# A causal convolution and a three-way maxout FFN in one kernel: merged tail blocks, six weight staging buffers, casts moved to GpSimd, and a new order of the stages

## The chip, the cores and the metric

The kernel runs on one core of a Trainium2 chip. The metric is the device time of one execution in microseconds (us); lower is better. Spans in the profile are about 2 us shorter than the measured time.

Engine names: PE is TensorE, DVE is VectorE, ACT is ScalarE, POOL is GpSimd, SP is SyncE (it only issues transfers here).

## The reference

```python
# x (8, 4160, 192) f32, weight (8, 7); moe_w1..w3 (192, 768), moe_w_out (768, 192)
w = softmax(weight, axis=-1)                              # 8 heads x 7 taps
# causal depthwise convolution, one 7-tap filter per head of 24 channels
out = einsum('hk,bskhg->bshg', w, windows_of_7(x))        # (8, 4160, 192)
x = out.reshape(33280, 192)
h = maximum(maximum(x @ w1, x @ w2), x @ w3)              # (33280, 768)
return h @ w_out                                          # (33280, 192)
```

4160 is 8 x 512 + 64.

## The kernel before

Work goes in blocks of up to 512 rows. For each block:

1. A transfer brings x in, and ACT casts it to fp16.
2. PE does the convolution as 40 small matmuls against a band matrix (5 chunks of 122 rows, 8 heads) into two PSUM tiles, G1 and G2. ACT casts both to fp16 (xctA, xctB).
3. Stage 1: six slices `j` of 128 hidden columns. Each slice takes six 128x512 matmuls into three PSUM tiles. ACT copies the first, and DVE takes two maxima.
4. Stage 2 of the *previous* block: four subtiles of 128 rows, six matmuls each. ACT copies the result out.

```python
    psg = ctx.enter_context(tc.tile_pool(name="psg", bufs=2, space=bass.MemoryType.PSUM))
    ps1 = ctx.enter_context(tc.tile_pool(name="ps1", bufs=4, space=bass.MemoryType.PSUM))
    ps2 = ctx.enter_context(tc.tile_pool(name="ps2", bufs=2, space=bass.MemoryType.PSUM))
    ...
            stage = wpool.tile([P, DFF], FP32, tag="wstage")      # one buffer, used six times
            nc.vector.memset(stage[:], 0.0)
            ...                                                   # 4 loads into stage
            nc.scalar.copy(out=wt[:], in_=stage[:])
    ...
    for t, (b, S, N) in enumerate(blocks):        # 72 blocks: 8 x (8 of 512 rows, 1 of 64)
        ...                                       # load x, nc.scalar.copy to x16
        ...                                       # 40 convolution matmuls into G1, G2
        nc.scalar.copy(out=xctA[:, 0:N], in_=G1[:, 0:N])
        nc.scalar.copy(out=xctB[:, 0:N], in_=G2[:, 0:N])
        if prev is not None:
            emit_stage2(prev)
        hT = htp.tile([P, NJ, NBLK], FP16, tag="hT")
        for j in range(NJ):
            ...                                   # 6 matmuls into psw[0..2]
            nc.scalar.copy(out=t1[:, 0:N], in_=psw[0][:, 0:N])
            nc.vector.tensor_max(out=t12[:, 0:N], in0=t1[:, 0:N], in1=psw[1][:, 0:N])
            nc.vector.tensor_max(out=hT[:, j, 0:N], in0=t12[:, 0:N], in1=psw[2][:, 0:N])
        prev = (hT, b, S, N)
```

The order of the source is not quite the order on the engines. A scheduler places the instructions when the kernel is built, and each engine then has its own list.

The softmax here doesn't subtract the row's maximum and nothing guards it: scores larger than these inputs give would overflow.

## Time and profile before

| before | value | read from |
|---|---|---|
| time | 806.5 us, median of 4 (806.11 to 807.0) | the times |
| PE busy / DVE busy / ACT busy | 92% / 68% / 55% | the page, part 1 |
| a batch (8 full blocks and a tail) | 94.7 us mean | ACT's casts of G in the timeline |
| its tail of 64 rows | 5.9 us | the same |
| a full block | 11.1 us mean | (94.7 - 5.9) / 8 |
| one slice on PE / on DVE | 1.296 / 1.39 us | the timeline |

From the page of before: the span; the busy times in us, with their share of the span and the number of instructions (PEld is the weight load); and the busy tenths of PE and DVE in 40 slices of 20 us.

```profile
span 804.3 us, 17219 instructions
...
PE 738.2 (92%) x6800; PEld 402.8 (50%) x6800; DVE 543.3 (68%) x943; ACT 439.6 (55%) x945; POOL 0.4 (0%) x5
...
PE   1279999999999999999999999999999999999997
...
DVE  7247766766676677676676667667766666766775
```

PE looks full after the first 40 us. It is not: a 128x512 matmul is drawn 0.38 us long but in an unbroken run the next starts 0.216 us later (402.54 and 402.75 below). The first three digits (1, 2, 7) are the slow start.

The timeline of before, across the end of one full block and the start of the next (start, duration, engine, line, operation, tiles; in brackets the idle time before it and who ended it):

```profile
402.33 0.68 DVE L266 TENSOR_TENSOR t<-t,psw 128x512 f32<-128x512 f32 x1
...
402.54 0.38 PE L249 MATMUL psw<-xctA,wt 128*128 128x512 f16 x1
...
402.75 0.38 PE L256 MATMUL psw<-xctB,wt 128*128 128x512 f16 x1
...
403.07 0.38 PE L249 MATMUL psw<-xctA,wt 128*128 128x512 f16 x1
...
403.12 0.69 DVE L267 TENSOR_TENSOR hT<-t,psw 128x512 f16<-128x512 f32 x1
...
403.72 0.68 DVE L266 TENSOR_TENSOR t<-t,psw 128x512 f32<-128x512 f32 x1
...
404.67 0.38 PE L256 MATMUL psw<-xctB,wt 128*128 128x512 f16 x1
...
404.98 0.65 PE L226 MATMUL G<-band,x 128*32 128x122 f16 x40
...
405.89 0.69 DVE L267 TENSOR_TENSOR hT<-t,psw 128x512 f16<-128x512 f32 x1
...
407.14 0.99 ACT L209 CAST x<-xf 128x960 f16<-128x960 f32 x1
...
408.46 0.61 ACT L265 COPY t<-psw 128x512 f32<-128x512 f32 x1
...
409.10 0.69 DVE L266 TENSOR_TENSOR t<-t,psw 128x512 f32<-128x512 f32 x1 [2.52 <-ACT t L265]
```

Two regimes alternate. Late in a block DVE runs without a gap: from 402.33 to 403.72 is one pair of maxima, 1.39 us, and PE, which could do a slice in 1.296, waits for PSUM that DVE has not freed: the matmul at 403.07 starts 0.32 us after the one before it, right after DVE's first maximum has ended at 402.33 + 0.68 = 403.01. Then, at 405.89, DVE finishes the last maximum, and it has nothing to do until 409.10. PE is busy with the convolution and with stage 2, and the first slice's copy by ACT comes only at 408.46. So each of the two engines limits the other for part of every block.

ACT's first casts of G around a tail block of before, from the timeline of ACT alone:

```profile
216.46 0.58 ACT L237 CAST xctA<-G 128x512 f16<-128x512 f32 x1 [0.96 <-PE G L226]
...
227.15 0.21 ACT L237 CAST xctA<-G 128x64 f16<-128x64 f32 x1 [0.53 <-PE G L226]
...
233.03 0.58 ACT L237 CAST xctA<-G 128x512 f16<-128x512 f32 x1 [0.31 <-PE G L226]
```

The tail's cast is at 227.15 and the next full block's at 233.03: 64 rows cost 5.9 us, more than half of what 512 rows cost.

The start of before, from the timeline:

```profile
28.57 0.70 DVE L117 MEMSET stage<- 128x768 f32 x1 [5.50 <-ACT wt L124]
...
33.38 0.83 ACT L124 CAST wt<-stage 128x768 f16<-128x768 f32 x1 [3.74 <-DMA stage<-in_moe_w_dram]
...
38.48 0.83 ACT L124 CAST wt<-stage 128x768 f16<-128x768 f32 x1 [4.27 <-DMA stage<-in_moe_w_dram]
...
43.63 0.83 ACT L124 CAST wt<-stage 128x768 f16<-128x768 f32 x1 [4.32 <-DMA stage<-in_moe_w_dram]
```

The weights pass through one staging buffer: a memset waits for the previous cast, then the load, then the cast, 5 us each time.

### The profile page before, as it was taken

Reading aid. Unit: us, or ns where it says so; the run is one execution under the profiler, and the core shown is the slowest. Engines: PE = TensorE matmul, PEld = TensorE weight load, DVE = VectorE, ACT = ScalarE, POOL = GpSimd, SP = SyncE. Lnnn points to the kernel's source line nnn. Section 1 sums busy time; section 2 is a strip of 40 time slices with the busy share of each in tenths; the row PEclk is TensorE's granted clock in tenths of the full one; section 3 lists DMA queues with packets and bytes.
Section 4 is the critical chain, followed back from the end, with each engine's and each line's share of the span. In section 5 each row is a group of like instructions: output and inputs, shape, how many; then the busy total and the mean of one; then the engine's idle time right before and its main releaser. Section 6 shows DMA issues by size and latency. Waiting matters only on the chain.

```text
span 804.3 us, 17219 instructions
## 1 busy us (share of the span) xinstructions
PE 738.2 (92%) x6800; PEld 402.8 (50%) x6800; DVE 543.3 (68%) x943; ACT 439.6 (55%) x945; POOL 0.4 (0%) x5
## 2 busy tenths in 40 slices
PE   1279999999999999999999999999999999999997
PEld 0135455455555555555554555555555555555544
DVE  7247766766676677676676667667766666766775
ACT  4335556555555555655555555555555555555544
POOL 0000000000000000000000000000000000000000
PEclk9999999999999999999999999999999999999999
DMA  7311322223132132213222222312222221230111
GB/s 192 95 30 44 86 89 90 71 67 90 52 110 66 46 89 89 76 62 89 90 89 72 67 72 64 117 47 65 90 89 73 66 88 52 94 103 26 40 41 42
DMA packets 78832, 60.73 MB, mean 76 GB/s; under 512 B 2880, under 2 KB 78176, under 8 KB 78752
## 3 DMA queue, kind: packets, MB, share of 16 engines
q1 hardware_dynamic: 78752, 59.64, 24.6%
q8 instruction: 53, 0.87, 0.4%
q14 instruction: 27, 0.22, 0.1%
HBM read 34.07 MB, written 25.56 MB: 74 GB/s over the span
## 4 chain that ended last, share of the span: by engine, by line
PE 81%; DVE 11%; issue 2%; ACT 2%; DMA 2%; SPq 1%; DVEq 0%; ACTq 0%
PE psw L249 33%; PE psw L256 31%; PE pso L168 14%; DVE hT L267 4%; DVE t L266 4%; PE G L226 2%; DVE bacc L97 2%; DMA stage<-in_moe_w_dram 2%; SPq L119 1%; ACT wt L124 1%; ACT xctB L238 1%; DMA wraw<-in_weight_dram 0%; ACT t L265 0%; DVE stage L117 0%; ACT out_sb L175 0%
## 5 line engine op out<-in xcount | busy, mean ns | idle before, releaser
L249 PE MATMUL psw<-xctA,wt 128*128 128x512 f16 (+1 forms) x1296 | 458.6, 360 | 12.3 <-ACT wt L124 9.8
L256 PE MATMUL psw<-xctB,wt 128*128 128x512 f16 (+1 forms) x1296 | 455.5, 359 | 8.1 <-ACT wt L124 8.1
L266 DVE TENSOR_TENSOR t<-t,psw 128x512 f32<-128x512 f32 (+1 forms) x432 | 272.2, 630 | 187.1 <-ACT t L265 135.6
L265 ACT COPY t<-psw 128x512 f32<-128x512 f32 (+1 forms) x432 | 235.7, 547 | 246.5 <-PE psw L256 232.8
L267 DVE TENSOR_TENSOR hT<-t,psw 128x512 f16<-128x512 f32 (+1 forms) x432 | 273.3, 635 | 46.8 <-PE psw L256 5.4
L256 PEld LDWEIGHTS <-wt 128*128 128x128 f16 x1296 | 124.3, 98 | 141.5 <-issue 23.9
L168 PE MATMUL pso<-wo,hT 128*128 128x192 f16 x1584 | 171.7, 247 | 23.5 <-DVE hT L267 22.7
L249 PEld LDWEIGHTS <-wt 128*128 128x128 f16 x1296 | 124.7, 98 | 132.7 <-ACT wt L124 10.8
L168 PEld LDWEIGHTS <-hT 128*128 128x128 f16 x1584 | 127.2, 98 | 58.0 <-DVE hT L267 34.7
L175 ACT COPY out_sb<-pso 128x192 f32<-128x192 f32 (+1 forms) x264 | 79.3, 322 | 30.6 <-PE pso L168 29.1
L226 PE MATMUL G<-band,x 128*32 128x122 f16 (+3 forms) x2624 | 66.3, 214 | 19.0 <-ACT band L105 18.0
L226 PEld LDWEIGHTS <-x 128*32 128x32 f16 (+2 forms) x2624 | 43.4, 97 | 65.9 <-issue 51.7
L237 ACT CAST xctA<-G 128x512 f16<-128x512 f32 (+1 forms) x72 | 39.1, 544 | 59.7 <-PE G L226 59.6
L209 ACT CAST x<-xf 128x960 f16<-128x960 f32 (+1 forms) x64 | 61.2, 960 | 0.7 <-DMA xf<-in_x_dram 0.5
L238 ACT CAST xctB<-G 128x512 f16<-128x512 f32 (+1 forms) x72 | 39.5, 550 | 0.7 <-PE G L226 0.7
L117 DVE MEMSET stage<- 128x768 f32 x6 | 4.2, 698 | 20.0 <-ACT wt L124 19.0
L97 DVE SCALAR_TENSOR_TENSOR bacc<-masks,wnrm,bacc 128x134 f32<-128x134 f32 x48 | 13.2, 350 | 0.0
L124 ACT CAST wt<-stage 128x768 f16<-128x768 f32 x6 | 5.0, 832 | 13.2 <-DMA stage<-in_moe_w_dram 12.8
L215 ACT CAST x<-xf 128x192 f16<-128x192 f32 (+2 forms) x24 | 8.4, 351 | 0.0
L105 ACT CAST band<-bacc 128x134 f16<-128x134 f32 x8 | 2.2, 302 | 4.1 <-DVE bacc L97 4.1
L133 ACT CAST wo<-wo_stage 128x1152 f16<-128x1152 f32 x1 | 1.2, 1152 | 2.7 <-DMA wo_stage<-in_moe_w_out_dram 2.7
L69 DVE TENSOR_REDUCE wsum<-wexp 128x8 f32<-128x56 f32 x1 | 0.2, 211 | 3.4 <-ACT wexp L67 3.4
(11 smaller groups left out, 6.5 us busy)
## 6 DMA issues: line engine op xcount, KB each, us to landing
out_dram<-out_sb SPq DMA_DIRECT2D x64, 384.0 KB
xf<-in_x_dram SPq DMA_DIRECT2D x48, 480.0 KB
xf<-in_x_dram SPq DMA_DIRECT2D x16, 384.0 KB
stage<-in_moe_w_dram SPq DMA_DIRECT2D x24, 72.0 KB
xf<-in_x_dram SPq DMA_DIRECT2D x8, 96.0 KB
wo_stage<-in_moe_w_out_dram SPq DMA_DIRECT2D x1, 576.0 KB
xf<-in_x_dram SPq DMA_DIRECT2D x8, 70.5 KB
xf<-in_x_dram SPq DMA_DIRECT2D x8, 52.5 KB
```

Of the source, the lines that this page charges most:

```text
L97: nc.vector.scalar_tensor_tensor(out=bacc[:], in0=masks[:, a, :], scalar=wnrm[:, h, k : k + 1], in1=bacc[:], op0=ALU.mult, op1=ALU.add,)
L168: nc.tensor.matmul(pso[0:ms, :], lhsT=hT[:, j, P * s : P * s + ms], rhs=wo[:, j, :], start=(j == 0), stop=(j == NJ - 1),)
L175: nc.scalar.copy(out=out_sb[0:ms, s, :], in_=pso[0:ms, :])
L209: nc.scalar.copy(out=x16[:, i : jx + 1, :], in_=xf32[:, i : jx + 1, :])
L226: nc.tensor.matmul(gt[32 * g : 32 * g + 32, out_lo:out_hi], lhsT=x16[0:rlen, q, cb : cb + 32], rhs=band[0:rlen, h, cc_lo : cc_lo + ncols], ...
L237: nc.scalar.copy(out=xctA[:, 0:N], in_=G1[:, 0:N])
L238: nc.scalar.copy(out=xctB[:, 0:N], in_=G2[:, 0:N])
L249: nc.tensor.matmul(psw[i][:, 0:N], lhsT=wg[i][0][:, P * j : P * (j + 1)], rhs=xctA[:, 0:N], start=True, stop=False,)
L256: nc.tensor.matmul(psw[i][:, 0:N], lhsT=wg[i][1][:, P * j : P * (j + 1)], rhs=xctB[:, 0:N], start=False, stop=True,)
L265: nc.scalar.copy(out=t1[:, 0:N], in_=psw[0][:, 0:N])
L266: nc.vector.tensor_max(out=t12[:, 0:N], in0=t1[:, 0:N], in1=psw[1][:, 0:N])
L267: nc.vector.tensor_max(out=hT[:, j, 0:N], in0=t12[:, 0:N], in1=psw[2][:, 0:N])
```

## The change

The intent: no small tail blocks, no serial start, and an order in which PE always has matmuls that wait for nobody. The core of the diff:

```diff
-            stage = wpool.tile([P, DFF], FP32, tag="wstage")
+            stage = wpool.tile([P, DFF], FP32, tag=f"wstage{i}{half}")
...
-    blocks: per batch 8 of 512 rows and 1 of 64
+    blocks: 64 of 512 rows, then one block made of the eight 64-row remainders (65 in all)
...
-                nc.scalar.copy(out=x16[:, i : jx + 1, :], in_=xf32[:, i : jx + 1, :])
+                nc.gpsimd.tensor_copy(
+                    out=x16[:, i : jx + 1, :], in_=xf32[:, i : jx + 1, :]
+                )
...
+    for t in range(NB):
+        emit_xdma(t + 3)                       # x three blocks ahead (4 buffers, 3 before)
+        ...
+        for ph in range(NJ):
+            emit_st1_j(t, ph)                  # slice ph of block t
+            if ph < nsub_prev:
+                emit_st2_sub(t - 1, ph, out_sb)   # subtile ph of block t - 1
+            lo = 0
+            hi = ncc if ph == 4 else 0
+            for ci in range(lo, hi):
+                emit_conv_chunk(t + 2, cchunks[ci], G1, G2)   # convolution of block t + 2
+        if G1 is not None:
+            emit_xg(t + 2, G1, G2)             # the two ACT casts of G
+        if t >= 1:
+            emit_out_dma(t - 1, out_sb)
```

(The two lines on blocks stand for a longer piece of code. In a slice the three weights are now used in the order 3, 1, 2. "The new order" below means all of the loop: convolution and x loads ahead, and stage 2 between the slices. In the changed kernel the casts of G are called xg.)

More of the change, by code (lines that the diff above doesn't have):

```diff
@@ L23 @@
 CHK = P - PAD
+NBLK = 512
 @with_exitstack
@@ L44, with conv_chunks @@
     NJ = DFF // P
-    NBLK = 512
-    NQMAX = ceil(NBLK / CHK)
+    blocks = []
+    nfull = SEQ // NBLK
+    for b in range(B):
+        for i in range(nfull):
+            blocks.append([(b, i * NBLK, NBLK, 0)])
+    segs = []
+    off = 0
+    for b in range(B):
+        s = nfull * NBLK
+        while s < SEQ:
+            n = min(SEQ - s, NBLK - off)
+            segs.append((b, s, n, off))
+            off += n
+            s += n
+            if off == NBLK:
+                blocks.append(segs)
+                segs = []
+                off = 0
+    if segs:
+        blocks.append(segs)
+    NB = len(blocks)
+    blkN = [sum(sg[2] for sg in blk) for blk in blocks]
+    def conv_chunks(blk):
+        res = []
+        q = 0
+        for (b, S, N, off) in blk:
+            qq = 0
+            while CHK * qq < N:
+                o_lo = CHK * qq
+                o_hi = min(o_lo + CHK, N)
+                row_lo = max(0, S + o_lo - PAD)
+                rlen = min(P, SEQ - row_lo)
+                cc_lo = o_lo - (row_lo - S)
+                res.append((q, b, row_lo, rlen, off + o_lo, off + o_hi, cc_lo))
+                q += 1
+                qq += 1
+        return res
+    NQMAX = max(len(conv_chunks(blk)) for blk in blocks)
     const = ctx.enter_context(tc.tile_pool(name="const", bufs=1))
     wpool = ctx.enter_context(tc.tile_pool(name="wpool", bufs=1))
-    xfp = ctx.enter_context(tc.tile_pool(name="xfp", bufs=3))
-    x16p = ctx.enter_context(tc.tile_pool(name="x16p", bufs=3))
-    xctp = ctx.enter_context(tc.tile_pool(name="xctp", bufs=2))
+    xfp = ctx.enter_context(tc.tile_pool(name="xfp", bufs=4))
+    x16p = ctx.enter_context(tc.tile_pool(name="x16p", bufs=4))
+    xgp = ctx.enter_context(tc.tile_pool(name="xgp", bufs=3))
     tmpp = ctx.enter_context(tc.tile_pool(name="tmpp", bufs=2))
@@ L128 @@
     wo_stage = wpool.tile([P, NJ, D], FP32)
-    nc.sync.dma_start(
-        out=wo_stage[:], in_=moe_w_out.rearrange("(j p) c -> p j c", p=P)
-    )
+    nc.sync.dma_start(out=wo_stage[:], in_=moe_w_out.rearrange("(j p) c -> p j c", p=P))
     wo = wpool.tile([P, NJ, D], FP16)
     nc.scalar.copy(out=wo[:], in_=wo_stage[:])
-    blocks = []
-    for b in range(B):
-        s = 0
-        while s < SEQ:
-            n = min(NBLK, SEQ - s)
-            blocks.append((b, s, n))
-            s += n
@@ L143 @@
-    out_2d = out
-    def conv_chunks(S, N):
-        res = []
-        q = 0
-        while CHK * q < N:
-            out_lo = CHK * q
-            out_hi = min(out_lo + CHK, N)
-            row_lo = max(0, S + out_lo - PAD)
-            rlen = min(P, SEQ - row_lo)
-            cc_lo = out_lo - (row_lo - S)
-            assert 0 <= cc_lo <= PAD and cc_lo + (out_hi - out_lo) <= BAND_W
-            res.append((q, row_lo, rlen, out_lo, out_hi, cc_lo))
-            q += 1
-        return res
-    def emit_stage2(prev):
-        hT, b, S, N = prev
-        gstart = b * SEQ + S
-        nsub = ceil(N / P)
-        out_sb = outp.tile([P, 4, D], FP32, tag="out_sb")
-        for s in range(nsub):
-            ms = min(P, N - P * s)
-            pso = ps2.tile([P, D], FP32, tag="ps2")
-            for j in range(NJ):
-                nc.tensor.matmul(
-                    pso[0:ms, :],
-                    lhsT=hT[:, j, P * s : P * s + ms],
-                    rhs=wo[:, j, :],
-                    start=(j == 0),
-                    stop=(j == NJ - 1),
-                )
-            nc.scalar.copy(out=out_sb[0:ms, s, :], in_=pso[0:ms, :])
-        nc.sync.dma_start(
-            out=out_2d[gstart : gstart + N, :].rearrange(
-                "(s p) c -> p s c", p=min(P, N)
-            ),
-            in_=out_sb[0 : min(P, N), 0:nsub, :],
-        )
@@ L183, with emit_xdma @@
-    prev = None
-    for t, (b, S, N) in enumerate(blocks):
-        chunks = conv_chunks(S, N)
-        nq = len(chunks)
-        xf32 = xfp.tile([P, NQMAX, D], FP32, tag="xf32")
-        x16 = x16p.tile([P, NQMAX, D], FP16, tag="x16")
+    out_2d = out
+    x16_t = {}
+    xg_t = {}
+    hT_t = {}
+    def emit_xdma(t):
+        if not (0 <= t < NB):
+            return
+        chunks = conv_chunks(blocks[t])
+        xf32 = xfp.tile([P, NQMAX, D], FP32, tag="xf32", name=f"xf32_{t}")
+        x16 = x16p.tile([P, NQMAX, D], FP16, tag="x16", name=f"x16_{t}")
+        x16_t[t] = x16
@@ L190 @@
         i = 0
-        while i < nq:
+        n = len(chunks)
+        while i < n:
             jx = i
             while (
-                jx + 1 < nq
-                and chunks[jx][2] == P
-                and chunks[jx + 1][2] == P
-                and chunks[jx + 1][1] - chunks[jx][1] == CHK
+                jx + 1 < n
+                and chunks[jx][3] == P
+                and chunks[jx + 1][3] == P
+                and chunks[jx + 1][1] == chunks[jx][1]
+                and chunks[jx + 1][2] - chunks[jx][2] == CHK
@@ L198 @@
             ):
                 jx += 1
-            (q0, row_lo0, rlen0, _, _, _) = chunks[i]
+            (q0, b0, row_lo0, rlen0, _, _, _) = chunks[i]
             cnt = jx - i + 1
@@ L204 @@
                     tensor=x.tensor,
-                    offset=(b * SEQ + row_lo0) * D,
+                    offset=(b0 * SEQ + row_lo0) * D,
                     ap=[[D, P], [CHK * D, cnt], [1, D]],
@@ L208 @@
                 nc.sync.dma_start(out=xf32[:, i : jx + 1, :], in_=src)
-                nc.scalar.copy(out=x16[:, i : jx + 1, :], in_=xf32[:, i : jx + 1, :])
+                nc.gpsimd.tensor_copy(
+                    out=x16[:, i : jx + 1, :], in_=xf32[:, i : jx + 1, :]
+                )
             else:
                 nc.sync.dma_start(
-                    out=xf32[0:rlen0, q0, :],
-                    in_=x[b, row_lo0 : row_lo0 + rlen0, :],
+                    out=xf32[0:rlen0, q0, :], in_=x[b0, row_lo0 : row_lo0 + rlen0, :]
@@ L214 @@
                 )
-                nc.scalar.copy(out=x16[0:rlen0, q0, :], in_=xf32[0:rlen0, q0, :])
+                nc.gpsimd.tensor_copy(out=x16[0:rlen0, q0, :], in_=xf32[0:rlen0, q0, :])
             i = jx + 1
-        G1 = psg.tile([P, NBLK], FP32, tag="g")
-        G2 = psg.tile([P, NBLK], FP32, tag="g")
-        for (q, row_lo, rlen, out_lo, out_hi, cc_lo) in chunks:
-            ncols = out_hi - out_lo
-            for h in range(NHEAD):
-                g = h % 4
-                gt = G1 if h < 4 else G2
-                cb = GRP * h if h < NHEAD - 1 else GRP * h - 8
-                nc.tensor.matmul(
-                    gt[32 * g : 32 * g + 32, out_lo:out_hi],
-                    lhsT=x16[0:rlen, q, cb : cb + 32],
-                    rhs=band[0:rlen, h, cc_lo : cc_lo + ncols],
-                    start=True,
-                    stop=True,
-                    tile_position=(0, 32 * g),
-                )
@@ L235 @@
-        xctA = xctp.tile([P, NBLK], FP16, tag="xctA")
-        xctB = xctp.tile([P, NBLK], FP16, tag="xctB")
-        nc.scalar.copy(out=xctA[:, 0:N], in_=G1[:, 0:N])
-        nc.scalar.copy(out=xctB[:, 0:N], in_=G2[:, 0:N])
-        if prev is not None:
-            emit_stage2(prev)
-        hT = htp.tile([P, NJ, NBLK], FP16, tag="hT")
-        for j in range(NJ):
-            psw = [
-                ps1.tile([P, NBLK], FP32, tag="ps1", name=f"psw{i}") for i in range(3)
-            ]
-            for i in range(3):
-                nc.tensor.matmul(
-                    psw[i][:, 0:N],
-                    lhsT=wg[i][0][:, P * j : P * (j + 1)],
-                    rhs=xctA[:, 0:N],
-                    start=True,
-                    stop=False,
-                )
-                nc.tensor.matmul(
-                    psw[i][:, 0:N],
-                    lhsT=wg[i][1][:, P * j : P * (j + 1)],
-                    rhs=xctB[:, 0:N],
-                    start=False,
-                    stop=True,
-                )
-            t1 = tmpp.tile([P, NBLK], FP32, tag="t1")
-            t12 = tmpp.tile([P, NBLK], FP32, tag="t12")
-            nc.scalar.copy(out=t1[:, 0:N], in_=psw[0][:, 0:N])
-            nc.vector.tensor_max(out=t12[:, 0:N], in0=t1[:, 0:N], in1=psw[1][:, 0:N])
-            nc.vector.tensor_max(
-                out=hT[:, j, 0:N], in0=t12[:, 0:N], in1=psw[2][:, 0:N]
-            )
@@ L271, with emit_conv_chunk @@
-        prev = (hT, b, S, N)
-    emit_stage2(prev)
+    def emit_conv_chunk(t, chunk, G1, G2):
+        x16 = x16_t[t]
+        (q, b, row_lo, rlen, out_lo, out_hi, cc_lo) = chunk
+        ncols = out_hi - out_lo
+        for h in range(NHEAD):
+            g = h % 4
+            gt = G1 if h < 4 else G2
+            cb = GRP * h if h < NHEAD - 1 else GRP * h - 8
+            nc.tensor.matmul(
+                gt[32 * g : 32 * g + 32, out_lo:out_hi],
+                lhsT=x16[0:rlen, q, cb : cb + 32],
+                rhs=band[0:rlen, h, cc_lo : cc_lo + ncols],
+                start=True,
+                stop=True,
+                tile_position=(0, 32 * g),
+            )
@@ new lines, in emit_xg, with emit_st1_j @@
+    def emit_xg(t, G1, G2):
+        N = blkN[t]
+        xg1 = xgp.tile([P, NBLK], FP16, tag="xg1", name=f"xg1_{t}")
+        xg2 = xgp.tile([P, NBLK], FP16, tag="xg2", name=f"xg2_{t}")
+        xg_t[t] = (xg1, xg2)
+        nc.scalar.copy(out=xg1[:, 0:N], in_=G1[:, 0:N])
+        nc.scalar.copy(out=xg2[:, 0:N], in_=G2[:, 0:N])
+    def emit_st1_j(t, j):
+        N = blkN[t]
+        (xg1, xg2) = xg_t[t]
+        jj = slice(P * j, P * (j + 1))
+        psw3 = ps1.tile([P, NBLK], FP32, tag="ps1", name=f"psw3_{t}_{j}")
+        psw1 = ps1.tile([P, NBLK], FP32, tag="ps1", name=f"psw1_{t}_{j}")
+        psw2 = ps1.tile([P, NBLK], FP32, tag="ps1", name=f"psw2_{t}_{j}")
+        nc.tensor.matmul(
+            psw3[:, 0:N], lhsT=wg[2][0][:, jj], rhs=xg1[:, 0:N], start=True, stop=False
+        )
+        nc.tensor.matmul(
+            psw3[:, 0:N], lhsT=wg[2][1][:, jj], rhs=xg2[:, 0:N], start=False, stop=True
+        )
+        nc.tensor.matmul(
+            psw1[:, 0:N], lhsT=wg[0][0][:, jj], rhs=xg1[:, 0:N], start=True, stop=False
+        )
+        nc.tensor.matmul(
+            psw1[:, 0:N], lhsT=wg[0][1][:, jj], rhs=xg2[:, 0:N], start=False, stop=True
+        )
+        nc.tensor.matmul(
+            psw2[:, 0:N], lhsT=wg[1][0][:, jj], rhs=xg1[:, 0:N], start=True, stop=False
+        )
+        nc.tensor.matmul(
+            psw2[:, 0:N], lhsT=wg[1][1][:, jj], rhs=xg2[:, 0:N], start=False, stop=True
+        )
+        t3 = tmpp.tile([P, NBLK], FP32, tag="t3", name=f"t3_{t}_{j}")
+        t12 = tmpp.tile([P, NBLK], FP32, tag="t12", name=f"t12_{t}_{j}")
+        nc.scalar.copy(out=t3[:, 0:N], in_=psw3[:, 0:N])
+        nc.vector.tensor_max(out=t12[:, 0:N], in0=t3[:, 0:N], in1=psw1[:, 0:N])
+        nc.vector.tensor_max(out=hT_t[t][:, j, 0:N], in0=t12[:, 0:N], in1=psw2[:, 0:N])
@@ new lines, in emit_st2_sub @@
+    def emit_st2_sub(t, s, out_sb):
+        N = blkN[t]
+        ms = min(P, N - P * s)
+        if ms <= 0:
+            return
+        hT = hT_t[t]
+        pso = ps2.tile([P, NBLK], FP32, tag="ps2", name=f"pso_{t}_{s}")
+        for j in range(NJ):
+            nc.tensor.matmul(
+                pso[0:ms, 0:D],
+                lhsT=hT[:, j, P * s : P * s + ms],
+                rhs=wo[:, j, :],
+                start=(j == 0),
+                stop=(j == NJ - 1),
+            )
+        nc.scalar.copy(out=out_sb[0:ms, s, :], in_=pso[0:ms, 0:D])
@@ new lines, in emit_out_dma @@
+    def emit_out_dma(t, out_sb):
+        for (b, S, n, off) in blocks[t]:
+            g0 = b * SEQ + S
+            if off == 0 and n == blkN[t]:
+                nc.sync.dma_start(
+                    out=out_2d[g0 : g0 + n, :].rearrange("(s p) c -> p s c", p=P),
+                    in_=out_sb[:, 0 : ceil(n / P), :],
+                )
+            else:
+                s = off // P
+                p0 = off % P
+                assert p0 + n <= P, "segment straddles a token subtile"
+                nc.sync.dma_start(
+                    out=out_2d[g0 : g0 + n, :].rearrange("(s p) c -> p s c", p=n),
+                    in_=out_sb[p0 : p0 + n, s : s + 1, :],
+                )
@@ new lines @@
+    for u in (0, 1, 2):
+        emit_xdma(u)
+    for u in (0, 1):
+        if u < NB:
+            g1 = psg.tile([P, NBLK], FP32, tag="g", name=f"G1_{u}")
+            g2 = psg.tile([P, NBLK], FP32, tag="g", name=f"G2_{u}")
+            for ch in conv_chunks(blocks[u]):
+                emit_conv_chunk(u, ch, g1, g2)
+            emit_xg(u, g1, g2)
+    for t in range(NB):
+        N = blkN[t]
+        emit_xdma(t + 3)
+        hT_t[t] = htp.tile([P, NJ, NBLK], FP16, tag="hT", name=f"hT_{t}")
+        out_sb = None
+        if t >= 1:
+            out_sb = outp.tile([P, 4, D], FP32, tag="out_sb", name=f"outsb_{t-1}")
+        G1 = G2 = None
+        cchunks = []
+        if (t + 2) < NB:
+            G1 = psg.tile([P, NBLK], FP32, tag="g", name=f"G1_{t+2}")
+            G2 = psg.tile([P, NBLK], FP32, tag="g", name=f"G2_{t+2}")
+            cchunks = conv_chunks(blocks[t + 2])
+        ncc = len(cchunks)
+        nsub_prev = ceil(blkN[t - 1] / P) if t >= 1 else 0
+        for ph in range(NJ):
[8 more added lines that the diff above has]
+            emit_xg(t + 2, G1, G2)
+        if t >= 1:
+            emit_out_dma(t - 1, out_sb)
+        hT_t.pop(t - 1, None)
+        xg_t.pop(t, None)
+        x16_t.pop(t - 1, None)
@@ L277 @@
+    out_sb = outp.tile([P, 4, D], FP32, tag="out_sb", name=f"outsb_{NB-1}")
+    for s in range(ceil(blkN[NB - 1] / P)):
+        emit_st2_sub(NB - 1, s, out_sb)
+    emit_out_dma(NB - 1, out_sb)
 _INS = ['x', 'weight', 'moe_w1', 'moe_w2', 'moe_w3', 'moe_w_out']
```

## The prediction

> **What bounds it now.** The page gives PE 92% busy, but pipelined matmuls overlap (0.38 us each, issued every 0.216 us), so that overstates. The Trainium skill says the same ("Perfetto Trace Analysis", Identifying the Most-Contended Engine). In the timeline a full block of 512 rows takes 11.2 us (ACT casts of G at 193.55, 204.86, 216.46). PE's own work in it is 36 x 0.216 = 7.8 us (stage 1), 24 x 0.083 = 2.0 (stage 2), 0.67 (40 convolution matmuls with the switch): 10.4 us. The rest is a hand-over: at each block start DVE sits idle about 2.5 us (2.52, 2.81 us, behind the ACT copy), then runs back to back at 1.39 us per slice (0.68 + 0.69), slower than PE's 1.296, so PE waits for PSUM late in the block. The 64-row tail block of each batch costs another 5.9 us. A batch is 94.9 us. Stage 1 only runs freely from about 52 us: six weight loads share one staging buffer, 5 us each.
>
> **What the change does.**
> - Tails: the eight 64-row blocks become one 512 block; 72 blocks become 65. Saves about 8 x 5.9 - 11 = 36 us.
> - Order: convolution two blocks ahead, one stage 2 subtile after each of slices 0 to 3, convolution after slice 4. PE then spends 1.8 us on five slices in six, DVE needs 1.39: DVE (8.3 us per block) and ACT (6 us) keep up, and the 2.5 us DVE hole goes.
> - Still lost: in the built order ACT does both casts of G (2 x 0.585) before the copy of slice 5. They wait for the convolution, so that copy ends about 2.0 us after it instead of 1.3, and PE, with four stage 1 PSUM buffers, should stall about 0.5 us in the next block's slice 0. Estimated period: 10.4 + 0.5 = 10.9 us.
> - Casts of x move from ACT (1.0 us per block) to POOL, with three blocks of lead. The steady DVE maxes read one SBUF and one PSUM operand; the Trainium skill ("SBUF — State Buffer", Who interferes with whom) says such an instruction does not contend with GpSimd; the trace of before can't show it, POOL being idle there.
> - Staging: six buffers. Stage 1 should start near 28 us (the DVE band chain ends at 22; memsets, friction, two convolutions and casts follow).
>
> **Sum.** 28.5 start + 9.7 first block + 62 x 10.9 + two blocks without convolution 19.5 + last stage 2 and output 6.5 = 740 span, and 2 us to the measured time: 742 us, range 718 to 766. All of it is on the critical path: about 22 us from the start, 36 from the tails, the rest from the order. Chances: faster by over 2% 0.96, within 2% 0.03, slower 0.01.
>
> **What would show it.** Starts of ACT's first cast of G 10.9 us apart; a PE wait of 0.3 to 0.7 us per block in slice 0, for ACT's copy or DVE's max; DVE about 75% busy; first stage 1 matmul before 30 us; POOL casts 1 to 3 us, awaited by nobody; maxes still 0.68 us.
>
> **What would make it wrong.** No stall in slice 0: period 10.4, time about 712. Maxes slowed by POOL's casts to over 0.8 us: DVE becomes the bound, 770 or more. POOL casts near 10 us: POOL bounds. Stage switches on PE costing 0.1 us each, ten per block: 60 us more. A start still near 45 us: 758.

## More of the kernel before

All runs that this document compares are fast, with a granted TensorE clock of 0.996 to 1.0.

The view of waits of before (engine, line, who was waited for: total us, times, longest):

```profile
DVE t L266 <- ACT t L265: 135.6, 85, 2.9
```

The DVE holes at the block starts are in this line: 85 waits, 1.6 us in the mean and at most 2.9.

## The result, and the profile after

| | before | after |
|---|---|---|
| time, median | 806.55 us (13 runs, 806.11 to 807.09) | 732.79 us (8 runs, 731.41 to 735.29) |
| ratio of fast runs | | 0.9085, 95% interval 0.9075 to 0.9094 |
| full block | 11.1 us | 10.68 us |
| remainders of 64 rows | 8 x 5.9 us | one block of 512 rows |
| block 0, slice 5 copied at | 54.66 us | 38.51 us |

A ratio is the mean time of one kernel's fast runs over that of the other's fast runs of the same rounds, so it is not quite the ratio of the medians quoted. The output is correct.

The page after, the same lines as before:

```profile
span 730.4 us, 16461 instructions
...
PE 695.4 (95%) x6524; PEld 386.6 (53%) x6524; DVE 552.0 (76%) x859; ACT 383.9 (53%) x797; POOL 72.8 (10%) x93
...
PE   0699999999999999999999999999999999999996
...
DVE  8677777777777777777777777777777777777774
```

The slow start is down to one slice, PE is at 95% of a shorter span, and POOL now has 10%.

The waits after:

```profile
DVE t L270 <- ACT t L269: 120.2, 256, 1.1
```

DVE's waits for ACT's copy are still 120 us in total, but they are 256 short ones of at most 1.1 us instead of 85 holes of up to 2.9. With DVE at 76% load, these short waits alone do not show a loss.

The timeline after, around the end of a block (slice 5 starts at 400.59, slice 0 of the next block at 401.89):

```profile
400.00 0.65 PE L225 MATMUL G<-band,x 128*32 128x122 f16 x40
...
400.59 0.39 PE L249 MATMUL psw<-xg,wt 128*128 128x512 f16 x1
...
400.70 0.58 ACT L239 CAST xg<-G 128x512 f16<-128x512 f32 x1 [0.87 <-PE G L225]
...
401.18 0.59 ACT L240 CAST xg<-G 128x512 f16<-128x512 f32 x1
...
401.66 0.60 ACT L269 COPY t<-psw 128x512 f32<-128x512 f32 x1
...
401.89 0.38 PE L249 MATMUL psw<-xg,wt 128*128 128x512 f16 x1
...
402.30 0.69 DVE L270 TENSOR_TENSOR t<-t,psw 128x512 f32<-128x512 f32 x1 [0.95 <-ACT t L269]
...
402.75 0.25 PE L281 MATMUL pso<-wo,hT 128*128 128x192 f16 x1
...
403.04 0.38 PE L261 MATMUL psw<-xg,wt 128*128 128x512 f16 x1
...
403.09 0.69 DVE L271 TENSOR_TENSOR hT<-t,psw 128x512 f16<-128x512 f32 x1
...
403.47 0.62 PE L281 MATMUL pso<-wo,hT 128*128 128x192 f16 x5
```

This is the place that the prediction pointed at. ACT does both casts of G (L239, L240) and only then the copy of slice 5 (L269), at 401.66, although the two matmuls that it reads are drawn as ended at 401.19. DVE's first maximum of slice 5 therefore ends at 402.99, and PE's matmul at 403.04 (L261) had to wait for the PSUM tile that this maximum reads. It started 0.29 us after the single stage 2 matmul at 402.75, which needs only 0.083. Summed over the slices of this block: slice 5 takes 1.30 us, slice 0 takes 2.03 instead of 1.79, slices 1 to 3 1.79 each, slice 4 with the convolution 1.97, in all 10.67.

POOL's cast and DVE's maximum at the same time, from the same timeline:

```profile
411.34 0.69 DVE L271 TENSOR_TENSOR hT<-t,psw 128x512 f16<-128x512 f32 x1
...
411.53 0.99 POOL L207 CAST x<-xf 128x960 f16<-128x960 f32 x1 [9.57 <-issue]
```

A maximum with one operand in SBUF and one in PSUM takes 0.69 us with a POOL cast beside it, as without.

The start after:

```profile
17.50 2.39 POOL L214 CAST x<-xf 128x192 f16<-128x192 f32 x1 [16.44 <-DMA xf<-in_x_dram]
...
19.54 1.29 DVE L132 TENSOR_SCALAR bacc<-masks,wnrm 128x134 f32<-128x134 f32 x2
...
28.17 0.61 PE L249 MATMUL psw<-xg,wt 128*128 128x512 f16 x1
```

Stage 1 starts at 28.17. Here POOL and DVE do meet. The POOL cast of 128x192 takes 2.39 us (0.35 us in the steady state), and two DVE operations that took 0.48 us take 1.29 while POOL casts run. The cost to the band chain is about 0.8 us in this run. It isn't the same in each run: in that of experiment 7 the chain is 3.0 us longer than in before (17.6 instead of 14.6 us).

### How the sum came out

| term of the prediction | predicted | measured |
|---|---|---|
| stage 1 starts | 28.5 | 28.2 |
| first block | 9.7 | 10.6 |
| 62 blocks | 62 x 10.9 = 676 | 62 x 10.68 = 662.3 |
| two blocks without convolution | 19.5 | 19.7 |
| last stage 2 and output | 6.5 | 9.7 |
| span | 740 | 730.4 |

The end took 3.2 us more than predicted: the last block is now the merged one, whose output leaves in eight separate transfers, issued one after the other in 5 us (the line is from the timeline of the last 16 us). Of the 3.2 us these transfers are about 2.3: with the merged block elsewhere the time from the last output copy to the end falls from 5.9 to 3.6 us (experiment 11).

```profile
722.96 5.01 SPq L302 DMA_DIRECT2D out_dram<-outsb  x8
```

### The profile page after: what moved, and what is told of

The parts are those of the page before. It is cut to its first block, busy times and chain, and to the rows that moved or that the text cites. A ratio compares the mean times of both kernels' runs of the same rounds, so it can differ in the third digit from the quotient of the medians.

```text
span 730.4 us, 16461 instructions
## 1 busy us (share of the span) xinstructions
PE 695.4 (95%) x6524; PEld 386.6 (53%) x6524; DVE 552.0 (76%) x859; ACT 383.9 (53%) x797; POOL 72.8 (10%) x93
## 4 chain that ended last, share of the span: by engine, by line
PE 95%; DVE 3%; DMA 1%; issue 1%; ACT 1%; ACTq 0%; DVEq 0%
PE pso L281 18%; PE psw L261 13%; PE psw L249 12%; PE psw L252 12%; PE psw L255 11%; PE psw L258 11%; PE psw L264 11%; PE G L225 5%; DVE bacc L137 2%; DMA wraw<-in_weight_dram 1%; DVE bacc L132 0%; ACT wt L164 0%; DVE t L270 0%; DVE wnrm L114 0%; DVE hT L271 0%
## 5 line engine op out<-in xcount | busy, mean ns | idle before, releaser
L270 DVE TENSOR_TENSOR t<-t,psw 128x512 f32<-128x512 f32 x390 | 267.4, 686 | 127.5 <-ACT t L269 120.2
L271 DVE TENSOR_TENSOR hT<-t,psw 128x512 f16<-128x512 f32 x390 | 268.0, 687 | 40.7
L269 ACT COPY t<-psw 128x512 f32<-128x512 f32 x390 | 229.5, 588 | 51.9 <-PE psw L252 21.4
L288 ACT COPY outsb<-pso 128x192 f32<-128x192 f32 x260 | 82.6, 318 | 215.9 <-PE pso L281 215.9
L281 PE MATMUL pso<-wo,hT 128*128 128x192 f16 x1560 | 184.3, 246 | 0.9 <-DVE hT L271 0.6
L261 PE MATMUL psw<-xg,wt 128*128 128x512 f16 x390 | 147.9, 379 | 2.3
L249 PE MATMUL psw<-xg,wt 128*128 128x512 f16 x390 | 148.7, 381 | 0.0
L252 PE MATMUL psw<-xg,wt 128*128 128x512 f16 x390 | 148.1, 380 | 0.0
L255 PE MATMUL psw<-xg,wt 128*128 128x512 f16 x390 | 148.1, 380 | 0.0
L258 PE MATMUL psw<-xg,wt 128*128 128x512 f16 x390 | 148.1, 380 | 0.0
L264 PE MATMUL psw<-xg,wt 128*128 128x512 f16 x390 | 147.8, 379 | 0.0
L207 POOL CAST x<-xf 128x960 f16<-128x960 f32 (+1 forms) x64 | 63.3, 991 | 493.2 <-PE G L225 424.8
L225 PE MATMUL G<-band,x 128*32 128x122 f16 (+3 forms) x2624 | 44.5, 211 | 25.5 <-ACT band L145 23.8
L239 ACT CAST xg<-G 128x512 f16<-128x512 f32 x65 | 38.0, 585 | 55.6 <-PE G L225 55.6
L264 PEld LDWEIGHTS <-wt 128*128 128x128 f16 x390 | 38.1, 98 | 49.9 <-issue 11.9
L255 PEld LDWEIGHTS <-wt 128*128 128x128 f16 x390 | 38.2, 98 | 46.2 <-issue 0.3
L258 PEld LDWEIGHTS <-wt 128*128 128x128 f16 x390 | 38.2, 98 | 46.1 <-issue 0.3
L261 PEld LDWEIGHTS <-wt 128*128 128x128 f16 x390 | 38.2, 98 | 46.0 <-issue 0.3
L249 PEld LDWEIGHTS <-wt 128*128 128x128 f16 x390 | 38.1, 98 | 10.4 <-issue 0.3
L252 PEld LDWEIGHTS <-wt 128*128 128x128 f16 x390 | 38.2, 98 | 8.3 <-issue 0.2
```

The costliest lines, as they stand in the source:

```text
L225: nc.tensor.matmul(gt[32 * g : 32 * g + 32, out_lo:out_hi], lhsT=x16[0:rlen, q, cb : cb + 32], rhs=band[0:rlen, h, cc_lo : cc_lo + ncols], ...
L249: nc.tensor.matmul(psw3[:, 0:N], lhsT=wg[2][0][:, jj], rhs=xg1[:, 0:N], start=True, stop=False)
L252: nc.tensor.matmul(psw3[:, 0:N], lhsT=wg[2][1][:, jj], rhs=xg2[:, 0:N], start=False, stop=True)
L255: nc.tensor.matmul(psw1[:, 0:N], lhsT=wg[0][0][:, jj], rhs=xg1[:, 0:N], start=True, stop=False)
L258: nc.tensor.matmul(psw1[:, 0:N], lhsT=wg[0][1][:, jj], rhs=xg2[:, 0:N], start=False, stop=True)
L261: nc.tensor.matmul(psw2[:, 0:N], lhsT=wg[1][0][:, jj], rhs=xg1[:, 0:N], start=True, stop=False)
```

## The experiments

Twelve kernels ran, each timed in three rounds against the kernel before on the same chip. In all of them the output was correct. "Before plus" is the kernel before with one part of the change; "after minus" is the changed kernel with one part taken back.

### 1. Before plus six staging buffers

```diff
-            stage = wpool.tile([P, DFF], FP32, tag="wstage")
+            stage = wpool.tile([P, DFF], FP32, tag=f"wstage{i}{half}")
```

> The kernel before with one edit: six weight staging buffers instead of one shared one. My theory: the start is bound by the serial weight loads, so slice work starts near 30 us and block 0 ends about 17 us earlier; time 787 to 791, and the steady blocks stay at 11.1 us. Rival: the start is bound by the band chain on DVE or by the x loads now queued behind 24 weight loads, and the time moves by less than 8 us.

Measured: 789.14 us against 806.78, ratio 0.9783 (0.9766 to 0.9799). Slice 5 of block 0 is copied at 37.41 us instead of 54.66, and a batch takes 94.4 us (94.7 before). The serial loads were the bound of the start; the prediction's share of 22 us was too large by four.

### 2. Before plus merged tails, first try

The old order of the loop, one staging buffer, ACT casts, three x buffers, the merged block.

> The kernel before with only the eight 64-row tails merged into one 512 block (old order, one staging buffer, ACT casts, three x buffers). My theory: eight tails of 5.9 us go and one block of 11.1 comes, 36 us off: 769 to 773. Rival: a tail block lets DVE catch up and so shortens its neighbours (10.7 to 10.8 us beside 11.2 to 11.3), so removing tails gives back some of it: 775 to 782.

Measured: 788.55 us, ratio 0.9776 (0.9761 to 0.979), outside both ranges. Its trace shows a flaw in the experiment: the slices used the weights in the order 3, 1, 2 of the changed kernel, and with one staging buffer the third weight loads last, so the first stage 1 matmul ran at 46.55 us. Steady blocks took 11.23 us. Experiment 10 repeats it, and shows that this flaw had cost only about 2 us.

### 3. Before plus casts of x on POOL

```diff
-                nc.scalar.copy(out=x16[:, i : jx + 1, :], in_=xf32[:, i : jx + 1, :])
+                nc.gpsimd.tensor_copy(out=x16[:, i : jx + 1, :], in_=xf32[:, i : jx + 1, :])
```

> The kernel before with only the x casts moved from ACT to POOL (four x buffers instead of three). My theory: the cast (1.0 us) sits on ACT at the block start, in the 2.5 us DVE hole, but the first copy there waits for its matmul anyway, so it gains 0 to 0.25 us a block: 791 to 806. Rival: the hole is made by the cast; taking it away gives about 0.5 us a block or more, 770 to 780.

Measured: 804.56 us, ratio 0.9974 (0.9959 to 0.9989). The 2.2 us are a difference of two: a batch takes 94.0 us instead of 94.7 (8 batches: 5.6 us), and slice 5 of block 0 comes 3.3 us later (57.98 instead of 54.66), with DVE's TENSOR_SCALAR of 128x134 at a mean of 684 ns instead of 283 in the band chain. POOL helps the steady state a little and hurts the start.

### 4. Before plus the new order

Convolution two blocks ahead and interleaved stage 2, with the eight tails kept, one staging buffer and ACT casts.

> Only the new order (convolution two blocks ahead, stage 2 subtiles between slices) with the eight tails separate, one staging buffer and ACT casts. My theory: full blocks go from 11.1 to about 10.7 to 10.9 us and tail blocks from 5.9 to about 4: 760 to 785. Rival: without the POOL cast or the merged tails the order gains nothing, over 795.

Measured: 767.37 us, ratio 0.9514 (0.95 to 0.9529): 39 us, more than half of the whole gain, although its start is 4.5 us later than before's (slice 5 of block 0 is copied at 59.12), mostly, it seems, for the reason of experiment 2: the last weight is cast only 0.9 us later (49.64 instead of 48.75). A batch is 89.2 us: 8 full blocks of 10.68 and a tail of 3.7. The order alone brings the full block to its final value, with the casts of x still on ACT, and makes the tails cheap too. No run takes the order apart, so what the convolution ahead and the interleaved stage 2 give by themselves stays open.

### 5. After minus the new order

```diff
-    (the interleaved loop)
+        conv of block t; casts of G; all of stage 2 of block t - 1; slices 0 to 5 of block t
```

(In words. The x loads, too, go back to the block that uses them.)

> The changed kernel with the old order put back (convolution and casts of the same block, then all of stage 2, then stage 1); merged tail, six staging buffers and POOL casts stay. Theory now: the order is the largest part, 45 us as the trace of the run with only the order shows (0.44 us on each of 64 full blocks, 2.2 on each of 8 tails), but here there are no tails, so 65 blocks at 11.2 instead of 10.7: 760 to 768. The shares of the prediction (start 22, tails 36, order the rest) would put it at 738 to 753.

Measured: 767.75 us, ratio 0.9526 to before (0.9508 to 0.9543), 35 us worse than the changed kernel; blocks of 11.23 us. The waits of this run:

```profile
DVE t L270 <- ACT t L269: 182.9, 65, 5.6
```

65 holes, one a block, mean 2.8 us: the DVE hole is back although the cast of x is not on ACT, so the hole belongs to the order and not to the cast. The shares that the prediction gave (order "the rest") were wrong, and this run is outside them.

### 6. After minus the casts on POOL

> The changed kernel with the x casts back on ACT. Theory: ACT then carries about 7 us of a 10.7 us block and has room, but the cast sits right behind the copy of slice 5 and ahead of the copy of slice 0, so slice 0 may stall up to 0.3 us more a block: 731 to 750. Rival: taking the cast off ACT is what made the order work: over 755.

Measured: 734.83 us against 806.47, ratio 0.9111 (0.9097 to 0.9124); steady blocks of 10.68 us with few exceptions. With ratios of 0.9111 and 0.9085 the cast on POOL is worth 2 us at most: the exceptions are four blocks of 11.04 us, and four such blocks also stand in the trace of experiment 9, where POOL does the casts. ACT has room for it.

### 7. After, convolution moved behind slice 5

```diff
-            hi = ncc if ph == 4 else 0
+            hi = ncc if ph == 5 else 0
```

> The changed kernel with the convolution emitted after slice 5 instead of slice 4; in the built order ACT then does the copy of slice 5 before both casts of G. Theory: the only stall left, 0.24 us in slice 0, comes from that copy being late; it goes, the period is 10.43 to 10.47 us and the time 717 to 721. Rival: the 0.24 us is the cost of PE changing between stages there: 731 to 735, period 10.68.

Measured: 717.71 us, ratio to before 0.8898 (0.8885 to 0.8911); against the changed kernel 15 us less. The period is 10.44 us. From its timeline:

```profile
404.47 0.58 ACT L269 COPY t<-psw 128x512 f32<-128x512 f32 x1 [0.71 <-PE psw L252]
...
405.23 0.65 PE L225 MATMUL G<-band,x 128*32 128x122 f16 x40
...
405.81 0.39 PE L249 MATMUL psw<-xg,wt 128*128 128x512 f16 x1
...
405.93 0.58 ACT L239 CAST xg<-G 128x512 f16<-128x512 f32 x1 [0.87 <-PE G L225]
...
406.89 0.60 ACT L269 COPY t<-psw 128x512 f32<-128x512 f32 x1
...
406.90 0.38 PE L264 MATMUL psw<-xg,wt 128*128 128x512 f16 x1
...
407.12 0.66 PE L281 MATMUL pso<-wo,hT 128*128 128x192 f16 x6
```

The copy of slice 5 is at 404.47, before the convolution and before the casts. The last matmul of slice 0 is followed by all six of stage 2's first subtile without a gap. 10.44 us is what PE's own work adds up to: 36 x 0.216 + 24 x 0.083 + 0.67 for the convolution.

A late copy has not gone; it has moved. Now slice 0 starts at 405.81 and its copy, behind the two casts, at 406.89. That is 1.08 us after the start of the slice, as late as the copy of slice 5 was in the changed kernel (401.66 - 400.59 = 1.07). But slice 0 is followed by six matmuls of stage 2, 0.5 us of work for PE, and slice 5 was followed at once by slice 0, so the same lateness costs nothing here. Slice 5 gains twice: its copy comes before the casts, and the convolution stands between it and slice 0. The run doesn't separate the two.

### 8. After minus the merged tails

> The changed kernel with the eight 64-row tails as blocks of their own again. Theory: a tail costs 3.7 us in the new order, so eight tails less one full block less about 3.5 us of eight serial output transfers at the very end: 746 to 750. Rival (the prediction's 5.9 us a tail): 765 to 769.

Measured: 745.11 us, ratio 0.9237 (0.9224 to 0.9251). This is 1 us below my range. A batch is 88.76 us, so a tail costs 88.76 - 8 x 10.68 = 3.3 us here. In the new order merging the tails is worth 12 us. Alone, in the old order, it is worth 21 (experiment 10): what a part is worth depends on the others.

### 9. After with five PSUM buffers for stage 1

```diff
-    ps1 = ctx.enter_context(tc.tile_pool(name="ps1", bufs=4, space=bass.MemoryType.PSUM))
-    ps2 = ctx.enter_context(tc.tile_pool(name="ps2", bufs=2, space=bass.MemoryType.PSUM))
+    ps1 = ctx.enter_context(tc.tile_pool(name="ps1", bufs=5, space=bass.MemoryType.PSUM))
+    ps2 = ctx.enter_context(tc.tile_pool(name="ps2", bufs=1, space=bass.MemoryType.PSUM))
```

> The changed kernel with five PSUM buffers for stage 1 and one for stage 2 (eight banks in all, as now); the built order of ACT stays, both casts of G ahead of the copy of slice 5. Theory: PE waits in slice 0 only because the buffer that it needs is held by slice 5 whose copy is late; a fifth buffer lets it go on, period 10.43 to 10.5, time 717 to 722, as with the convolution moved. Rival: what cost the time was the late copy itself or the interleaved stage 2 matmul, not the buffer: 730 to 734. If one buffer for stage 2 is too few, a new wait on the out copy appears and the time rises above 735.

Measured: 733.39 us, ratio 0.9083 (0.9069 to 0.9096); no gain, and my theory of the wait fell. From its timeline, at the same place of a block:

```profile
402.15 0.60 ACT L269 COPY t<-psw 128x512 f32<-128x512 f32 x1
...
402.79 0.69 DVE L270 TENSOR_TENSOR t<-t,psw 128x512 f32<-128x512 f32 x1 [0.96 <-ACT t L269]
...
403.46 0.38 PE L264 MATMUL psw<-xg,wt 128*128 128x512 f16 x1
...
403.58 0.69 DVE L271 TENSOR_TENSOR hT<-t,psw 128x512 f16<-128x512 f32 x1
403.68 0.91 PE L281 MATMUL pso<-wo,hT 128*128 128x192 f16 x6
```

The three PSUM tiles of slice 0 now come without a wait (the last matmul, L264, is at 403.46). But the six matmuls of stage 2's first subtile take 0.91 us instead of 0.66: the sixth reads the columns of slice 5, and DVE finishes these only at 403.58 + 0.69 = 404.27. The period is still 10.68 us. Two waits were lined up behind the one late copy; the fifth buffer removed the first, and the second takes the same time. What experiment 7 changed was where the late copy falls.

### 10. Before plus merged tails, mended

Experiment 2 with the weights used in the order 1, 2, 3.

> The run with only the tails merged, mended: its slices began with the third weight, which loads last when one staging buffer is shared, and its stage 1 started about 7 us late; here the slices use the weights in the order 1, 2, 3 again. Theory: about 7 us less than that run, 779 to 784, with blocks still at 11.23 us, so 22 to 27 us gained and not 36: the full blocks lose the two cheap neighbours (10.7 us) of a tail, and the eight small output transfers end the run. Rival: the 36 us come back: 769 to 773.

Measured: 786.86 us against 807.73, ratio 0.9744 (0.973 to 0.9759). This is above both ranges, about 3 us above mine: 21 us gained and not 36. The mend gave 2 us and not 7: slice 5 of block 0 is copied at 57.54 instead of 59.46. The trace accounts for the 21. 65 blocks of 11.23 us are 730; 8 batches of 94.7 were 758, so the steady part gains 28. A full block without tails near it costs 11.23, not the mean of 11.1 that the tails had made possible: next to a tail a block takes 10.7 to 10.8, probably because a tail lets DVE catch up. Against this, slice 5 of block 0 comes 2.9 us later than in before, as the last weight is cast 3.1 us later (51.84 instead of 48.75), and the end has the exposed last stage 2 of a full block and eight transfers.

### 11. The best version: convolution behind slice 5, merged block in the middle

```diff
+    blocks.insert(len(blocks) // 2, blocks.pop())
     NB = len(blocks)
...
-            hi = ncc if ph == 4 else 0
+            hi = ncc if ph == 5 else 0
```

> The changed kernel with the convolution after slice 5 and the merged tail block placed in the middle instead of last. Theory: the end loses the eight serial output transfers, 3 to 4 us less than with the moved convolution alone: 713 to 715. Rival: the end is hidden or the merged block costs the same anywhere: 717 to 719.

Measured: 714.93 us, ratio 0.8854 (0.8841 to 0.8868), as expected, and with the next run the fastest of all; the quotient of this ratio and the changed kernel's, 0.8854 / 0.9085, puts it 2.5% below the changed kernel. The time from the last output copy's end to the end of the span is 3.6 us instead of 5.9. Of the 3.1 us between the profiled runs of 7 and 11, 2.2 lie in the end and 0.9 before block 1, which starts earlier here (39.65 instead of 40.55 us); the edit doesn't touch that part.

### 12. The same with an easier start

As 11, with the staging memsets on POOL and the first three blocks' casts on ACT.

> As best1, and the start eased: staging memsets on POOL instead of DVE, and the casts of the first three x blocks on ACT instead of POOL, so that POOL and the DVE band chain do not meet. Theory: the band chain ends about 1.7 us earlier (DVE TENSOR_SCALAR mean back from 384 to 283 ns) and slice work starts about 2 us earlier: 711 to 713. Rival: the meeting of POOL and DVE costs nothing on the chain and the time stays within 1 us of best1.

Measured: 715.09 us, ratio 0.8858 (0.8843 to 0.8873): no difference from 11. The experiment did not do what it should: the POOL cast of the fourth block moved forward into the band chain (2.07 us long), DVE's TENSOR_SCALAR stayed at 386 ns, and the weight loads, now behind the x loads, held up the first slices (slice 5 of block 0 at 39.23 instead of 38.16). So no run removes the meeting of POOL and DVE at the start and leaves the rest as it was. Its cost to the band chain can be read from the traces alone: 0.8 us in the changed kernel, 3.0 in experiment 7, 3.2 in experiment 3.

### The parts side by side

| part | alone, added to before | taken out of after |
|---|---|---|
| six staging buffers | 17.6 us | not run |
| merged tails | 20.9 us | 12.3 us |
| casts on POOL | 2.2 us | 2.0 us |
| new order | 39.4 us | 35.0 us |

The four single gains add up to 80 us; together they give 73.8.

## Why the prediction was right, and where it was not

- **The time.** 742 us predicted, 732.8 measured, inside the range of 718 to 766. The gain was 64 us predicted and 74 measured. The predicted span was 9.6 us too long, net: the blocks took 14 us less than predicted, and the first block and the end 4 us more.
- **What bounds it, and what the order does.** Right. DVE and PE took turns in holding each other up; the order cured that, and nothing else of the change did (experiments 1, 3, 4, 5 and 10).
- **The stall in slice 0.** Right in place and in the late copy, wrong in size. The prediction put the copy's end 2.0 us after the convolution; it is 402.26 - 400.59 = 1.67. It had added up durations of 0.585 us. Back to back, ACT starts such copies every 0.48 us (400.70, 401.18, 401.66). The stall is 0.24 us a block, not 0.5. With it the period is 10.68 us and not 10.9, which over 62 blocks is 14 us, more than the whole error. The Trainium skill has this: "ScalarE: Activation LUTs", What ACT_TABLE_LOAD costs, says that back-to-back ACTIVATEs overlap by about 93 ns, and this trace shows 0.58 - 0.48 = 0.10 us for ACT's casts. Two such overlaps are 0.2 of the 0.33 us. This is the term that was mis-sized.
- **The wait behind the stall.** The prediction blamed the four PSUM buffers. They were only the first of two waits on the same late copy (experiment 9).
- **The end.** 6.5 us predicted, 9.7 measured: it forgot that the merged block, being last, leaves in eight transfers (about 2.3 us of the 3.2).
- **The shares.** "About 22 us from the start, 36 from the tails, the rest from the order" was wrong. The rest would have been 6.5 us. Measured alone it is 18, 21 and 39. The total came out all the same because the sum was built from times of the new kernel and not from these shares. The tails were costed at what they cost in the old order, while the new order makes a tail cost 3.3 to 3.7 us instead of 5.9; and the full blocks were compared with 11.2 us each, which is not their mean next to tails.
- **POOL.** Right. 0.99 us a cast, waited for by nobody in the steady state, the maxima unchanged at 0.68 to 0.69 us. The Trainium skill ("SBUF — State Buffer", Who interferes with whom) says that a DVE instruction with at most one SBUF input, outside the 2-port perf modes (modes that use both of DVE's port pairs), does not contend with GpSimd; this trace agrees. The same section says that one with two SBUF inputs contends with a GpSimd instruction that reads SBUF. At the start DVE builds the bands with such instructions (SCALAR_TENSOR_TENSOR): beside them a cast took 2.39 us instead of 0.35, while twelve of them kept their 3.31 us; in the run of experiment 7 twelve of them took 6.11. The operation that took 1.29 us, TENSOR_SCALAR, reads a single tensor from SBUF and so is not that case; the section names it among those that can enter a 2-port mode, but no run here shows which mode it was in.
- **Matmuls.** The step of 0.216 us that all the sums used agrees with the Trainium skill ("TensorE: Matmul & The Clock Gate", Wait — 56ns, not 53.3ns?), which gives 215.7 ns for N = 512.

## What to carry to other kernels

When two engines are each loaded below 100% and yet both wait, look for the order in which they run rather than for time on either: here the new order, with the same 16461 instructions in the profile as the old one (experiment 5), was worth half of the gain. Where an engine keeps to its list, as ACT does here, ask for each instruction on the way to the bound engine what stands in front of it, whether that one waits, and how much other work the bound engine has before it needs the result: moving the convolution by one slice, one character of source, gave 15 us more. And a buffer that is waited for need not be a buffer that is missing; if another wait stands behind it on the same late producer, more buffers change nothing.

## What the Trainium skill lacked or had wrong

- "TensorE: Matmul & The Clock Gate", Back-to-back issue gap, says that in a stream of weight loads and matmuls the sustained spacing at N = 512 is about 131 ns, and that N/2.4 + 2.5 over-counts. The timelines have 0.21 to 0.22 us from start to start in a stream of exactly this kind (in that of after, matmuls at 404.14, 404.36, 404.57, 404.79 and 405.00, each with a weight load between); the formula was right (36 such steps and the rest add up to the period of 10.44 us).
- "TensorEngine Tiling (Array Packing)", Key Properties, says that changing the tiling mode drains the TensorE, and gives no cost. Here the step from a full-array matmul to the packed convolution is 0.31 us (404.67 to 404.98 in before) instead of 0.216, so 0.09 us more; that these are the drain is not shown. The whole group of 40 packed matmuls with both changes takes 0.67 us of PE (404.67 to 405.56, less one step of 0.216).
- "GPSIMD Engine Reference", Engine selection, calls one-input operations roughly line-rate, and no page gives a measured time for a cast on POOL. Here a cast of 128x960 from fp32 to fp16 took 0.99 us on POOL and 1.00 us on ACT.
